# Start of a fused attention and MLP kernel: diagonal table, v and q's sums of batch 0 issued sooner, the first weight's magnitudes in h's buffers, products of constants in TensorE's planned gaps

## The chip, the cores and the metric

The kernel runs on one NeuronCore of a Trainium2 chip. A core has five engines that run at the same time, each through a queue of its own in order: TensorE (PE, matrix products; its weight loads, PEld, overlap with them), VectorE (DVE), ScalarE (ACT), GpSimd (POOL) and SyncE (SP), which here issues all DMAs. They wait for one another through semaphores. The time is that of one execution on the device, in microseconds; the median of several executions counts. One further execution is recorded by the hardware profiler.

## The reference

For a batch of 8 and 8 heads of 576 tokens by 64, a Nystroem attention with 32 landmarks (means over 18 tokens each of q and k), its output as 512 columns x; then x plus the real part of a two-dimensional Fourier transform of x, a normalisation, and a two-layer MLP whose input is added again.

```
q_lm, k_lm = means of 18 tokens
A, Bm, C = softmax(q k_lm'), softmax(q_lm k_lm'), softmax(q_lm k')
Z = Bm' / (norms);  6 times: Z = 2 Z - Z Bm Z
x = A Z C v
u = x + Re(fft(fft(x, tokens), columns))
un = (u - mean) / sqrt(var + 1e-6)
out = u + relu(un @ w1) @ w2          # w1 512x2048, w2 2048x512
```

## The kernel before, in words

All products are of float16 pairs (a high and a low part, three products for one) or of float32. Two things have to happen before the MLP can run. The weights arrive as 64-bit floats: each weight has 16 pieces of 128 by 512. ACT forms a piece's magnitudes (`prepare`), DVE takes the float32 out of the bits in three instructions, ACT sums its magnitudes for a bound (the inner `bound`), and when all 16 have a bound, one scale for the weight is worked out (`scale`) and each piece is halved into high and low part (`halve`, ACT then DVE, in place, one slot below where it lay). And batch 0 has to go through the attention (`tokens`, `landmarks`), the transform (`mix`) and the normalisation (`norm`); its normalised rows are transposed by DMA into `unT`. The MLP (`mlp`) works on chunks of 256 rows: the first layer gives tiles `h`, the second (`second`) adds them up in two PSUM tiles `acc0` and `acc1`. The second layer of chunk 0 needs the halved second weight.

The program is a planner in Python (`run`): attention, weights and MLP are generators, taken in this order of priority, and each yields how long it means to wait. The planner keeps a time of its own, `now`, that moves on by the reckoned length of each product (`mm`, `tr`; at full clock) and, when every generator waits, jumps to the first that is due. What it emits is PE's order, fixed by hand (`manual_schedule`). The order on the other engines' queues is worked out afterwards by the framework, from the order of emission, the dependencies and its own reckoning of times, so an instruction emitted early may come later on its engine.

Loads: `load(0)`, called in the constructor, issues k and q of batch 0 for two groups of heads, then for each group `EARLY` = 4 pieces of the first weight and v. The other pieces are issued by `weights`, one ahead of `prepare`. The small constants are issued around it, the diagonal table `diag32` and the transform's tables (`t1`, `t1t`, `t2`) after it. The buffers `big` (8), `mid` (7), `row` (6) and `h` (4) are rings that several uses share; a new tile waits until an earlier one of its ring is free. In `tokens`, per group: DVE forms landmark sums `lm`, ACT sums of magnitudes of q (`amax`), and DVE the masked sums `qbd`; then a scale `kb`, a product with ones, and the splits of q. In `landmarks`, the table `diag32` enters where `nrm` is formed, and again in the first step of the iteration.

Of the kernel before, what the change touches and what calls it, by code (L numbers as in the profile page):

```python
# [2 lines left out]

# [1 line left out]

# [5 lines left out]
F32 = mybir.dt.float32  # L11
F16 = mybir.dt.float16
# [6 lines left out]
P = 128  # L19
# [3 lines left out]
SEG = 73  # L23
# [7 lines left out]
LAG = 2  # L31


AHEAD, PREP, EARLY = 1, 4, 4

MARGIN, NM, AM, M0 = 1.5, 2.0, 2.0, 0.2

# [90 lines left out]
class Kernel:  # L128
    def __init__(self, ctx, tc, NB, q, k, v, w1, w2, t1, t1t, t2, diag, mask, out):
        self.tc, self.nc, self.NB = tc, tc.nc, NB  # L130
        self.q, self.k, self.v, self.w1, self.w2, self.out = q, k, v, w1, w2, out
        nc = self.nc
        pool = lambda n, b: ctx.enter_context(tc.tile_pool(name=n, bufs=b))
        psum = lambda n, b: ctx.enter_context(tc.tile_pool(name=n, bufs=b, space=bass.MemoryType.PSUM))
        self.cp, self.wk, self.sm = pool("cp", 1), pool("wk", 1), pool("sm", 2)
        self.ps_at, self.ps_h, self.ps_o = psum("ps_at", 8 - PSH - TCH), psum("ps_h", PSH), psum("ps_o", 1)
        self.loads = {}
        self.now, self.there, self.read, self.used = 0.0, {}, {}, []
        self.V, self.A = Timed(self, nc.vector, 0.07, 1.04e-3, 0.52e-3), Timed(self, nc.scalar, 0.2, 0.83e-3, 0.83e-3)
        self.G = Timed(self, nc.gpsimd, 0.1, 2.6e-3, 2.8e-3)  # L140
        self.dma_free = 2.0

        def const(src, shape, dtype, name):
            t = self.cp.tile(shape, dtype, name=name)
            nc.sync.dma_start(t, src)
            return t

        self.wraw, self.raw_there = [], []
        self.whole = [self.cp.tile([P, NF + 1, 512], F32, name=f"w{w}") for w in range(2)]
        self.mask = const(mask, [P, 6], F32, "mask")  # L150
        self.load(0)
        self.mask4, self.mask2 = self.mask[:, 0:4], self.mask[:, 4:6]
        self.diag32 = const(diag, [P, 32], F32, "diag")
        self.ident = self.cp.tile([P, P], F32, name="ident")
        make_identity(nc, self.ident)
        self.ones = self.cp.tile([P, P], F32, name="ones")
        nc.vector.memset(self.ones, 1.0)
        self.ones16 = self.cp.tile([P, P], BF16, name="ones16")
        nc.vector.memset(self.ones16, 1.0)
        self.ones_bd = self.cp.tile([P, 4, 32], F32, name="ones_bd")  # L160
        nc.vector.tensor_copy(self.ones_bd, self.mask4.unsqueeze(2).broadcast_to([P, 4, 32]))
        self.mhalf = self.cp.tile([P, 2], F32, name="mhalf")
        nc.vector.memset(self.mhalf, -0.5)

        self.Wx = self.cp.tile([P, 2, 2, 256], F16, name="Wx")
        self.Wt = self.cp.tile([P, 2, 4, 64], F16, name="Wt")
        for t in (self.Wx, self.Wt):
            nc.gpsimd.memset(t, 0.0)
        self.t1 = const(t1, [P, 4, 2, 160], F16, "t1")
        self.t1t = const(t1t, [P, 2, 2, 320], F16, "t1t")  # L170
        self.t2 = const(t2, [P, 4, 2, 2, NC], F16, "t2")
        self.arrival(1.7)
# [40 lines left out]
    def split(self, hi, lo, src, scale):  # L213
        self.A.activation(hi, src, AF.Copy, scale=scale)
        self.V.scalar_tensor_tensor(lo, src, scale, hi, ALU.mult, ALU.subtract)
# [34 lines left out]
    def weights(self):  # L250
# [12 lines left out]
        def prepare(i):  # L263


            mag = self.row(512)
            A.activation(mag, self.wraw[i].rearrange("p (m x) -> p m x", x=2)[:, :, 1].bitcast(F32), AF.Abs, scale=2.0**-112)
            mags.append(mag)

        def bound(i):  # L270
# [104 lines left out]
    def tokens(self, b, st):  # L375
# [10 lines left out]
        for g in range(2):  # L386
            kf, qf = loads[g][0][:, 0 : 2 * S], loads[g][1][:, 0:NQ]
            V.tensor_reduce(lm[:, g, 64:128], kf.rearrange("p (m t) -> p m t", t=18), AX.X, ALU.add)

            lv = lm[:, g, 0:64].rearrange("p (x o m) -> p x o m", o=2, m=8)  # L390
            qv = qf.rearrange("p (x o t) -> p x o t", o=2, t=2 * SEG)
            for o in range(2):
                V.tensor_reduce(lv[:, :, o], qv[:, :, o, o : o + 144].rearrange("p x (m t) -> p x m t", t=18), AX.X, ALU.add)
            qhs.append(self.big().bitcast(F16))
            A.activation(qhs[g][:, 0:NQ], qf, AF.Abs, accum_out=am[:, g : g + 1])
            for h2 in range(2):
                ms, cols = self.mask2[:, h2 : h2 + 1], slice(32 * h2, 32 * h2 + 32)
                V.tensor_scalar(
                    qbd[:, 2 * g : 2 * g + 2, cols], lm[:, g, 0:64].rearrange("p (r m) -> p r m", r=2), ms, None, ALU.mult
                )  # L400
            yield self.till(qbd)
# [4 lines left out]
        eq, rq = self.power(am[:, 0:2], 2, 2.0**-13, "aq")  # L406
        kb = self.small(2, "kb", BF16)
        V.tensor_tensor(kb, am[:, 2:4], eq, ALU.mult)
        yield self.till(kb, more=AM)
        ek, rk = self.bound(kb, 2, 2.0**-13, "ak")  # L410
        sc = self.small(4, "sc")
# [6 lines left out]
        for h2 in range(2):  # L418
# [2 lines left out]
                kbd[..., cols].rearrange("p g y r m -> p (g y r) m"), klm.rearrange("p g y (r m) -> p (g y r) m", r=2),  # L421
                ms, None, ALU.mult,
            )
        qm = [h[:, 0:2048].rearrange("p (y r t) -> p y r t", y=2, r=2) for h in qhs]
        qr = [h[:, 2048:2304].rearrange("p (y r t) -> p y r t", y=2, r=2) for h in qhs]
        for g in range(2):
            qs = loads[g][1][:, 0:NQ].rearrange("p (x t) -> p x t", t=2 * SEG)
            for t, a, w in ((qm[g], 1, 128), (qr[g], 129, 16)):
                split(
                    *(t[:, y].rearrange("p r (s t) -> p (r s) t", t=w) for y in range(2)),  # L430
                    qs[:, :, a : a + w], rq[:, g : g + 1],
                )
            if g == 0:
                yield self.till(qhs[0], kbd)
        while b == 1 and self.seconds < NF // 2 - HB:
            yield 0.5

# [275 lines left out]
    def mix(self, b, st, WC, Wx, x2, x13):  # L713
# [5 lines left out]
        for nt in range(3):  # L719
# [44 lines left out]
            if nt < 2 or b2 == 1:  # L764
                yield from self.norm(b, uts)

    def u_tile(self):
        self.ulive += 1
        return self.wk.tile([P, DM], F32, name="u", bufs=UB)
# [64 lines left out]
    def mlp(self):  # L834
# [4 lines left out]

        def second(ch, i, h):  # L840
            if i == 0:
                acc[:] = [self.ps_o.tile([P, DM], F32, name=f"acc{t}") for t in range(TCH)]
            while self.split_w[1] < 2 * i + 2:
                yield 0.5
            yield self.till(h)
            for t in range(TCH):
                for x in range(2):
                    f = 2 * i + x
                    mm3(acc[t], lambda y: h[:, y, x, P * t : P * t + P], lambda y: self.w2s[f][:, y, :],
                        start=(f == 0), stop=(f == NF - 1))  # L850
                    yield 0.0
                if f == NF - 1:
                    u = self.utiles[TCH * ch + t]
                    V.scalar_tensor_tensor(u, acc[t], self.inv2, u, ALU.mult, ALU.add)
                    nc.sync.dma_start(self.out[(TCH * ch + t) * P : (TCH * ch + t + 1) * P, :], u)
                    self.ufree.append(self.now + 4.5)

            self.seconds += 1

        for ch in range(self.NB // 2 * 9 // TCH):  # L860
# [6 lines left out]
            for i in range(NF // 2):  # L867
                while self.split_w[0] < 2 * i + 2:
                    yield 0.5
                ps = self.ps_h.tile([P, 512], F32, name="h")  # L870
                for x in range(2):
                    for c in range(KT):
                        mm3(ps[:, n * x : n * x + n], lambda y: self.w1s[2 * i + x][:, y, c, :], lambda y: unT[:, y, c, :],
                            start=(c == 0), stop=(c == KT - 1))
                        if c % 2:
                            yield 0.0
                if ch > 0 or i >= NF // 2 - HB:
                    h = self.wk.tile([P, 2, 2, n], F16, name="h", bufs=HB)
                else:

                    h = self.mid().bitcast(F16)[:, 0 : 4 * n].rearrange("p (y x t) -> p y x t", y=2, x=2)
                hv = [h[:, y].rearrange("p x t -> p (x t)") for y in range(2)]
                A.activation(hv[0], ps, AF.Relu)
                V.scalar_tensor_tensor(hv[1], ps, 0.0, hv[0], ALU.max, ALU.subtract)
                while len(late) >= LAG and (ch > 0 or self.split_w[1] >= 2 * late[0][1] + 2):
                    yield from second(*late.pop(0))
                late.append((ch, i, h))
# [14 lines left out]
    def run(self):  # L902
# [9 lines left out]
        with self.tc.manual_schedule(engines={mybir.EngineType.PE}):  # L912
            while self.threads:
# [6 lines left out]
                            self.threads.remove(th)  # L920
                        break
                else:
                    self.now = min(t[1] for t in self.threads)
                assert self.now < 5000


# [65 lines left out]
```

## Time and profile before

| | us |
|---|---|
| median of 3 executions | 1054.99 |
| lowest, highest | 1053.08, 1055.08 |
| the profiled execution | 1054.7 |
| its span, first to last instruction | 1052.9 |
| PE busy | 966.5 |
| DVE busy | 627.3 |
| ACT busy | 347.3 |
| POOL busy | 146.7 |

The page gives busy time by engine, then 40 slices of the span (a digit is the busy share in tenths; PEclk is the clock granted to PE in tenths of full speed), the DMA queues, the chain that ended last, and groups of instructions. Other views of the same trace give an engine's waits, the instructions in order of time, and busy times for chosen stretches. The line numbers that instructions carry are mostly those of helpers (L123 for DVE, ACT and POOL, L201 and L206 for PE), so instructions are told apart by their tiles, written "out<-in". "at" is any PSUM tile of the attention; "w" the weights, "wsc" their scales, "wm" a weight's maximum.

### The profile page before, as it was taken

How to read it: one execution, taken by the hardware profiler on the slowest of the kernel's cores; microseconds unless marked ns; L12 is line 12 of the kernel's file. 1: busy time of each engine (PE TensorE's matmuls, PEld its weight loads, DVE VectorE, ACT ScalarE, POOL GpSimd, SP SyncE). 2: the span in 40 equal slices, each digit the busy share in tenths (PEclk: the TensorE clock that was granted, in tenths of full speed). 3: DMA queues.
4: the chain of work that ended last, by engine and by line, in shares of the span. 5: the costliest groups of instructions: out<-in, count | busy, mean ns of one | idle time of the engine just before them, and what ended most of it. 6: DMA issues, size and time to landing. Idle time of an engine off the chain costs nothing.

```text
span 1052.9 us, 19418 instructions
## 1 busy us (share of the span) xinstructions
PE 966.5 (92%) x7900; PEld 666.3 (63%) x7900; DVE 627.3 (60%) x1684; ACT 347.3 (33%) x771; POOL 146.7 (14%) x161
## 2 busy tenths in 40 slices
PE   1556678899999999999999999999999999999998
PEld 0434434567776677766776677767766677676665
DVE  7888898779553665538745674687451754441111
ACT  3567755333231422223332332233222322111110
POOL 0101102034011030112302130214010130110000
PEclk8577889999999999999999999999999999999999
DMA  9564412123411123112502250125021110120000
GB/s 324 183 220 141 136 48 94 45 42 58 162 21 31 37 69 135 21 31 46 177 9 50 36 168 17 46 41 167 28 41 21 46 24 21 21 50 21 1 21 21
DMA packets 102122, 75.63 MB, mean 72 GB/s; under 512 B 72464, under 2 KB 90896, under 8 KB 101904
## 3 DMA queue, kind: packets, MB, share of 16 engines
q1 hardware_dynamic: 102032, 74.39, 25.0%
q8 instruction: 62, 1.02, 0.4%
q14 instruction: 28, 0.23, 0.1%
HBM read 48.02 MB, written 9.44 MB: 55 GB/s over the span
## 4 chain that ended last, share of the span: by engine, by line
PE 81%; DVE 10%; issue 4%; ACT 3%; DMA 1%; POOL 1%; SPq 0%; POOLq 0%; ACTq 0%; DVEq 0%
PE h L201 34%; PE acc L201 33%; PE at L201 14%; DVE w L123 2%; DVE mid L123 1%; DVE row L123 1%; DVE lm L123 1%; ACT mid L123 1%; DVE big L123 1%; ACT w L123 1%; DMA big<-q_dram 1%; ACT big L123 1%; DVE asum L123 0%; DMA unT<-row 0%; POOL mid L123 0%
## 5 line engine op out<-in xcount | busy, mean ns | idle before, releaser
L201 PE MATMUL h<-unT,w 128*128 128x256 f16 x3456 | 416.9, 275 | 16.8 <-DVE w L123 7.5
L201 PEld LDWEIGHTS <-w 128*128 128x128 f16 x3456 | 337.4, 99 | 92.6 <-DVE w L123 10.6
L201 PE MATMUL acc<-w,h 128*128 128x512 f16 x1680 | 393.6, 380 | 0.0
L201 PEld LDWEIGHTS <-h 128*128 128x128 f16 x1680 | 162.7, 98 | 163.3 <-issue 4.5
L123 DVE SCALAR_TENSOR_TENSOR h<-h 128x512 f16<-128x512 f32 x140 | 95.9, 685 | 205.3 <-ACT h L123 204.7
L123 ACT ACTIVATE h<-h 128x512 f16<-128x512 f32 x140 | 83.1, 594 | 287.4 <-PE h L201 275.4
L123 POOL TENSOR_TENSOR mid<-mid 128x256 f32<-128x256 f32 (+2 forms) x44 | 48.8, 1118 | 178.7 <-ACT mid L123 128.6
L123 POOL TENSOR_TENSOR r<-ve,mhalf 128x2 f32<-128x2 f32 (+1 forms) x20 | 13.8, 688 | 410.4 <-DVE ve L123 405.4
L123 POOL TENSOR_TENSOR row<-row 128x512 f16<-128x512 f32 (+1 forms) x44 | 47.7, 1100 | 43.2 <-ACT row L123 43.2
L123 DVE TENSOR_REDUCE lm<-big 128x32 f32<-128x576 f32 (+1 forms) x48 | 44.2, 945 | 13.9 <-DMA big<-k_dram 11.0
L201 PEld LDWEIGHTS <-mid 128*128 128x128 f16 x432 | 39.5, 102 | 19.1 <-issue 9.4
L123 ACT CAST row<-row 128x512 f16<-128x512 f32 (+1 forms) x44 | 23.3, 556 | 82.4 <-DVE row L123 82.2
L201 PEld LDWEIGHTS <-big 128*128 128x128 f16 (+1 forms) x768 | 41.5, 105 | 10.9 <-issue 2.2
L123 DVE TENSOR_TENSOR mid<-mid 128x256 f32<-128x256 f32 (+1 forms) x60 | 40.7, 693 | 12.2 <-DMA mid<-mid 9.7
L123 DVE SCALAR_TENSOR_TENSOR row<-at,scw,row 128x262 f32<-128x262 f32 (+1 forms) x48 | 21.4, 486 | 39.1 <-ACT row L123 19.2
L123 ACT ACTIVATE row<-w 128x512 f32<-128x512 f32 x54 | 33.8, 639 | 19.2 <-DMA w<-w_dram 9.8
L123 DVE SCALAR_TENSOR_TENSOR u<-at,scw,row 128x128 f32<-128x128 f32 (+3 forms) x120 | 39.0, 388 | 0.5 <-DMA out_dram<-u 0.5
L201 PE MATMUL at<-RE,E 128*128 128x96 f32 (+1 forms) x192 | 30.2, 281 | 8.3 <-DVE RE L123 8.3
L201 PEld LDWEIGHTS at<-RE,E 128*128 128x128 f32 x192 | 26.6, 196 | 14.2 <-DVE RE L123 6.0
L201 PE MATMUL at<-mid,big 128*128 128x262 f16 (+1 forms) x288 | 33.9, 288 | 0.0
L123 DVE SCALAR_TENSOR_TENSOR u<-acc,wsc,u 128x512 f32<-128x512 f32 x36 | 26.6, 747 | 11.8 <-PE acc L201 11.7
L123 POOL TENSOR_TENSOR mid<-mid,asum 128x512 f32<-128x512 f32 x14 | 15.2, 1090 | 123.6 <-DVE asum L123 113.3
(164 smaller groups left out, 932.8 us busy)
## 6 DMA issues: line engine op xcount, KB each, us to landing
w<-w_dram SPq DMA_DIRECT2D x22, 512.0 KB, 8.9
big<-v_dram SPq DMA_DIRECT2D x16, 640.0 KB, 9.2
big<-q_dram SPq DMA_DIRECT2D x16, 584.0 KB, 5.9
big<-k_dram SPq DMA_DIRECT2D x16, 576.0 KB, 4.5
out_dram<-u SPq DMA_DIRECT2D x36, 256.0 KB, 2.0
big<-w_dram SPq DMA_DIRECT2D x10, 512.0 KB, 6.1
unT<-row SPq DMA_TRANSPOSE x72, 2.5
t<-t_dram SPq DMA_DIRECT2D x1, 1048.0 KB, 9.5
```

The costliest lines, as they stand in the source:

```text
L123: return call(out, *args, **kw)
L201: self.nc.tensor.matmul(out, a, b, start=start, stop=stop, skip_group_check=True)
```

## The change

Five edits.

```
-AHEAD, PREP, EARLY = 1, 4, 4
+AHEAD, PREP, EARLY = 1, 4, 2
...
         self.mask = const(mask, [P, 6], F32, "mask")
+        self.diag32 = const(diag, [P, 32], F32, "diag")
         self.load(0)
         self.mask4, self.mask2 = self.mask[:, 0:4], self.mask[:, 4:6]
-        self.diag32 = const(diag, [P, 32], F32, "diag")
```

The diagonal table is issued ahead of batch 0's loads, and only two pieces of the first weight ahead of each v; the next four follow the tables.

```
-            mag = self.row(512)
-            A.activation(mag, self.wraw[i]..., AF.Abs, scale=2.0**-112)
+            mag = self.h_tile().rearrange("p y x t -> p (y x t)").bitcast(F32) if i < NF else self.row(512)
+            with self.tc.issue_after(self.first_sums) if i < NF // 2 else nullcontext():
+                A.activation(mag, self.wraw[i]..., AF.Abs, scale=2.0**-112)
...
-            A.activation(qhs[g][:, 0:NQ], qf, AF.Abs, accum_out=am[:, g : g + 1])
+            ins = A.activation(qhs[g][:, 0:NQ], qf, AF.Abs, accum_out=am[:, g : g + 1])
+            if b == 0:
+                self.first_sums = ins.ins
...
+    def h_tile(self):
+        return self.wk.tile([P, 2, 2, TCH * P], F16, name="h", bufs=HB)
```

The first weight's magnitudes use tiles of h's ring, and the first eight of them come on ACT's queue behind the sums of q of batch 0 that have been emitted by then. `mlp` takes its h tiles from `h_tile` too.

```
         V.tensor_tensor(kb, am[:, 2:4], eq, ALU.mult)
+        ... split_q(g): the two splits of group g, formerly in a loop behind kbd
+        split_q(0)
         yield self.till(kb, more=AM)
...
-        for g in range(2):
-            ...
-            if g == 0:
-                yield self.till(qhs[0], kbd)
+        split_q(1)
+        yield self.till(qhs[0], kbd)
```

The first half of q is split ahead of the product that kb is for, in every batch.

```
+        self.idle = self.cp.tile([P, 256], BF16, name="idle")
+        nc.vector.memset(self.idle, 1.0)
+        self.spare = self.ps_o.tile([P, DM], F32, name="acc0")
...
             if i == 0:
+                self.spare = None
                 acc[:] = [self.ps_o.tile([P, DM], F32, name=f"acc{t}") for t in range(TCH)]
...
                 else:
-                    self.now = min(t[1] for t in self.threads)
+                    until = min(t[1] for t in self.threads)
+                    while self.spare is not None and until - self.now > 0.25:
+                        self.mm(self.spare[:, 0:256], self.ones16, self.idle)
+                    self.now = until
```

Where the planner's time jumps by more than 0.25 us, products of a 128x128 tile of ones with 256 columns of ones are emitted for the time of the jump, into the PSUM tile that `acc0` uses later and that nobody reads until then. The last ones come before the second layer's first call.

More of the change, by code (lines that the diff above doesn't have):

```diff
@@ L1 @@
 import math
-from contextlib import ExitStack
+from contextlib import ExitStack, nullcontext
 import numpy as np
@@ L263, in prepare @@
         def prepare(i):
-            mag = self.row(512)
-            A.activation(mag, self.wraw[i].rearrange("p (m x) -> p m x", x=2)[:, :, 1].bitcast(F32), AF.Abs, scale=2.0**-112)
+            mag = self.h_tile().rearrange("p y x t -> p (y x t)").bitcast(F32) if i < NF else self.row(512)
+            with self.tc.issue_after(self.first_sums) if i < NF // 2 else nullcontext():
+                A.activation(mag, self.wraw[i].rearrange("p (m x) -> p m x", x=2)[:, :, 1].bitcast(F32), AF.Abs, scale=2.0**-112)
             mags.append(mag)
@@ L408, in tokens, with split_q @@
         V.tensor_tensor(kb, am[:, 2:4], eq, ALU.mult)
+        qm = [h[:, 0:2048].rearrange("p (y r t) -> p y r t", y=2, r=2) for h in qhs]
+        qr = [h[:, 2048:2304].rearrange("p (y r t) -> p y r t", y=2, r=2) for h in qhs]
+        def split_q(g):
+            qs = loads[g][1][:, 0:NQ].rearrange("p (x t) -> p x t", t=2 * SEG)
+            for t, a, w in ((qm[g], 1, 128), (qr[g], 129, 16)):
+                split(
+                    *(t[:, y].rearrange("p r (s t) -> p (r s) t", t=w) for y in range(2)),
+                    qs[:, :, a : a + w], rq[:, g : g + 1],
+                )
+        split_q(0)
         yield self.till(kb, more=AM)
@@ L423, in tokens @@
             )
-        qm = [h[:, 0:2048].rearrange("p (y r t) -> p y r t", y=2, r=2) for h in qhs]
-        qr = [h[:, 2048:2304].rearrange("p (y r t) -> p y r t", y=2, r=2) for h in qhs]
-        for g in range(2):
[L427 to L432, printed above, removed]
-            if g == 0:
-                yield self.till(qhs[0], kbd)
+        split_q(1)
+        yield self.till(qhs[0], kbd)
         while b == 1 and self.seconds < NF // 2 - HB:
@@ L877, in mlp @@
                 if ch > 0 or i >= NF // 2 - HB:
-                    h = self.wk.tile([P, 2, 2, n], F16, name="h", bufs=HB)
+                    h = self.h_tile()
                 else:
```

## The prediction

> **What bounds the kernel now.** I read the page's 40 slices first, to see where TensorE (PE) isn't full.
>
> ```profile
> span 1052.9 us, 19418 instructions
> PE   1556678899999999999999999999999999999998
> DVE  7888898779553665538745674687451754441111
> PEclk8577889999999999999999999999999999999999
> ```
>
> From the eighth slice on PE is full; before, it is half full at a reduced clock, and DVE is the fuller engine. The windows view prices those stages (columns: stretch, length, busy time of PE, weight loads, DVE, ACT and POOL, granted clock, DMA share, GB/s; the last row is the same view for DVE alone).
>
> ```profile
> 0.00:140.00 140.00, 73.75 (x568) 52.18 (x569) 118.15 (x301) 87.92 (x202) 14.64 (x19) 0.76 0.60 193
> 140.00:172.00 32.00, 23.30 (x157) 11.42 (x156) 26.95 (x88) 17.36 (x35) 0.00 (x0) 0.82 0.17 56
> 250.00:1053.00 803.00, 796.90 (x6551) 553.21 (x6548) 418.47 (x1110) 210.84 (x464) 113.32 (x122) 1.00 0.20 53
> 5.25:140.00 134.75, 117.61 (x297) 0.75 0.60 194
> ```
>
> After 250 us PE is busy 796.9 of 803 at full clock, with work that the change doesn't touch: an earlier start of that stage moves the end by as much, and nothing else does. Two views in order of time show when it can start.
>
> ```profile
> 139.64 0.16 DVE L123 TENSOR_REDUCE wm<-wmax 128x1 f32<-128x16 f32 x1
> 144.67 0.72 ACT L123 ACTIVATE w<-w,wsc 128x512 f16<-128x512 f32 x1 [4.35 <-DVE wsc L123]
> 158.32 0.72 ACT L123 ACTIVATE w<-w,wsc 128x512 f16<-128x512 f32 x1 [0.82 <-DVE w L123]
> 159.07 0.75 DVE L123 SCALAR_TENSOR_TENSOR w<-w,wsc 128x512 f16<-128x512 f32 x1 [0.79 <-ACT w L123]
> 170.07 0.72 ACT L123 ACTIVATE w<-w,wsc 128x512 f16<-128x512 f32 x1 [1.27 <-DVE w L123]
> ```
>
> The maximum of the second weight is taken at 139.64, when its last piece is decoded. Then its pieces are halved one after another, ACT waiting for DVE and DVE for ACT (each writes a slot that the one before still reads), to 170.07: a chain of some 25 us (170.07 - 144.67) that hangs on 139.64 and that no edit shortens. Up to 139.64 DVE sets the pace: from its first load (5.25) to 140 it works 117.61 of 134.75 us. So the gain, if there is one, is what goes of DVE's 134.75 - 117.61 = 17.1 us of idle time. Its waits up to 140, by the view of waits (us in total, times, longest):
>
> ```profile
> DVE mid L123 <- ACT mid L123: 3.1, 2, 1.9
> DVE row L123 <- POOL row L123: 2.6, 2, 1.6
> DVE w L123 <- ACT w L123: 2.0, 2, 1.8
> DVE cmx L123 <- PE at L201: 1.4, 3, 0.5
> DVE wm L123 <- PE at L201: 1.1, 1, 1.1
> DVE RE L123 <- PE at L201: 0.7, 1, 0.7
> DVE E L123 <- PE at L201: 0.7, 1, 0.7
> DVE row L123 <- ACT row L123: 0.5, 1, 0.5
> DVE amx L123 <- PE at L201: 0.4, 1, 0.4
> ```
>
> **The change part by part.** *The multiplied constants.* Wherever the planner leaves PE idle for over 0.25 us before the second layer begins, products of 256 columns of ones fill the gap. What that buys is the clock.
>
> ```profile
> 12.62 0.43 PE L201 MATMUL at<-lm,qbd 128*64 128x32 f32 x4 [2.92 <-DVE qbd L123]
> 12.86 4.09 PE L201 MATMUL at<-big,qbd 128*64 128x288 f32 x16
> 235.06 2.14 PE L201 MATMUL at<-big,qbd 128*64 128x288 f32 x16
> 95.23 4.58 PE L201 MATMUL h<-unT,w 128*128 128x256 f16 x23 [0.83 <-DMA unT<-row]
> 226.40 2.62 PE h L201 x24
> 99.00:100.00 1.00, 1.00 (x13) 0.71 (x12) 0.00 (x0) 0.15 (x1) 0.38 (x1) 0.92 0.00 0
> 43.00:44.00 1.00, 0.59 (x6) 0.42 (x4) 0.94 (x6) 0.60 (x1) 0.00 (x0) 1.00 0.00 0
> 45.00:46.00 1.00, 0.73 (x4) 0.76 (x5) 1.00 (x6) 0.00 (x0) 0.29 (x1) 0.50 0.00 0
> ```
>
> The same 16 products take 4.09 us early and 2.14 later: the early ones ran at half clock, though the page's first slice shows 8. A product of 256 columns takes 4.58 / 23 = 0.20 us slow and 2.62 / 24 = 0.11 fast; the fast clock comes some 4 us into a burst (95.23 to 99) and was gone again at 45, with PE some 0.6 busy at 43. If PE stays fast, DVE's waits on it shrink. The two waits on "mid" (3.1 us) stand behind first-layer bursts like that of 95.23, which shortens by half its 4.58; I take 2.5 (from 0 to 3.1). Those on E, wm and RE at 60 us (0.7, 1.1, and shares of the small ACT copies between, the 0.5 of row among them) stand behind short products; of the 2.3 I take 1.9 (0 to 2.3). Those on RE at 37 us and amx (0.7 + 0.4) stand behind the scores: 0.8 (0 to 1.1). Those on cmx (1.4) I count at 0 (below). Sum: 2.5 + 1.9 + 0.8 = 5.2 us gained, between 0 and 7.9.
>
> The page "TensorE: Matmul & The Clock Gate" of the Trainium skill (Part 1) has PE throttle only after a whole idle window of about 3.4 us and speed up after a busy one. By that rule PE should have stayed fast from 43 to 45, and few constants would do; the rows disagree, since a PE 0.6 busy was throttled there. The sum would be the same -5.2 by either.
>
> What the constants cost: their operand is set by DVE behind ones_bd.
>
> ```profile
> 2.52 0.23 DVE L161 COPY ones_bd<-mask 128x128 f32<-128x128 f32 x1 [1.37 <-DMA mask<-mask_dram]
> ```
>
> So PE can begin at about 2.52 + 0.23 + 0.2 = 2.9 us (the set of 128x256 taken at the size of that copy), in time in which DVE waits for its first load: nothing on DVE. But PE is then behind. Filling the 12.62 us before the first products that wait for DVE takes 12.62 / 0.11 = 115 constants: 25 of them slow (5 us at 0.20), 90 fast (9.9 us), so they end at 2.9 + 5 + 9.9 = 17.8, 5.2 us late. The 16 products behind then take 2.14 in place of 4.09, which leaves 3.2 us. I take that as hidden, since batch 0's chain has more slack than that (next part) and DVE has pieces to decode meanwhile; the gain on cmx is given up for it. Without that cover it is a rival. In all, at most (140 - 73.75) / 0.11 = 602 constants, 66 us of PE's idle time; none comes after the second layer's first call, and the slow products there are covered by the halving chain (0; the bound is what the clock of 0.82 costs in the 32 us from 140 on, 0.18 x 32 = 5.8 us).
>
> *Diagonal table, q's sums, v.*
>
> ```profile
> 0.74 0.39 SPq L145 DMA_DIRECT2D mask<-mask_dram  x1
> 1.19 0.42 SPq L361 DMA_DIRECT2D big<-k_dram  x1
> 17.60 0.68 DVE L123 SCALAR_TENSOR_TENSOR w<-w,row 128x512 int32<-128x512 int32 x1
> 19.22 0.21 DVE L123 TENSOR_REDUCE rs<-nrm 128x2 f32<-128x64 f32 x1
> 25.66 1.16 ACT L123 ACTIVATE big<-big 128x1168 f16<-128x1168 f32 x1
> 28.59 0.14 DVE L123 TENSOR_TENSOR kb<-amax,aq_e 128x2 bf16<-128x2 f32 x1
> 29.72 0.22 DVE L123 TENSOR_TENSOR nrm<-diag,rs 128x64 f32<-128x64 f32 x1
> 36.23 1.08 PE L201 MATMUL at<-big,mid 128*32 128x64 f32 x31
> 29.93 0.69 DVE L123 SCALAR_TENSOR_TENSOR w<-w,row 128x512 int32<-128x512 int32 x1
> ```
>
> The table now goes ahead of k and q on SP's queue: their issue moves by 1.19 - 0.74 = 0.45 us, and DVE's first work with it: +0.45. It landed so late that nrm waited from 19.4 (the end of rs) to 29.72, 10 us, and q's sums ran at 25.66, behind magnitudes of the first weight on ACT, so kb came at 28.59. With both early, batch 0's chain can run some 10 us sooner. That isn't 10 us of time: from 17.60 to 29.93 DVE decoded seven pieces, so it only does its work in another order. Next late in the place of table and sums are the splits of q (a pair on DVE for each half), of which the change takes the first half ahead of the wait for kb's product. I take 0; the bounds are -2 (a chain that is done sooner leaves fewer steps in which DVE waits) and the loss of the next point. v was needed at 36.23, behind a chain that started at 28.59; 10 us sooner it needs v1 at 26, which it gets, two pieces of weight being gone from ahead of each v: 0.
>
> The edge that holds the first eight magnitudes behind q's sums makes ACT wait for q: behind it stand those magnitudes, and DVE's decoding behind them. the second half of q is reduced and masked ahead of the products of 12.62, so two sums of 1.16 end at about 13 at the latest, and the first piece was decoded with the row of 17.60: 0, with 1.16 as the other end.
>
> *Four pieces later.* Pieces 4 to 7 of the first weight are issued behind v and the tables and not before v1, so the second v and all tables stand ahead of piece 4 now. By 30 us DVE had decoded seven pieces (17.60 is the end of the first, 29.93 that of the last), three of them from piece 4 on, each at most three rows like these: 3 x 3 x 0.69, up to 6.2 us of work in hand gone, against q's splits and the rest of batch 0's chain that are early now. I take 0; bounds 0 and +6.2.
>
> *Magnitudes in h's buffers.* Four buffers of their own in place of a share of six; ACT is busy 87.9 of 140 us and DVE waits 0.5 us for such a row: 0, from -0.5 to +1 (at most four in flight, not five).
>
> **Sum:** -5.2 + 0.45 = -4.7. The profiled execution took 1054.7 us (span 1052.9, 1.8 around it), 0.3 under the median of 1054.99: 1054.7 - 4.7 = 1050.0.
>
> **The rivals.** 0.2% is 2.1 us, about what a measurement can tell from no change.
>
> *The constants make PE late (slower).* PE takes its queue in order and every planned gap is full, so the 5.2 us by which the first constants run late are never made up: each later product starts as late against the plan. For: the count above; the planner reckons with full clock and constants from time 0, and the trace shows neither. Against: batch 0's chain was itself 10 us late. It decides from the point where DVE has no decoded piece ready and waits for a product. Then the gain is lost and 5.2 + 0.45 comes on top: 1060.4.
>
> *The waits change their owner.* DVE's queue has an order of its own; where PE is sooner, it waits for ACT or POOL instead (4 of the 9 rows above are theirs, 2.6 and 2.0 among them), or PE idles beyond the plan where DVE is late, and is slow again. By the page named above an idle window of 3.4 us would be enough for that; the trace's row at 45 says that less is enough. Gain and 0.45 cancel: 1054.5.
>
> *More holes close.* Batch 0's chain done early also takes the waits on POOL and ACT (2.6 + 2.0 + 0.5) and the 2 us of the chain's bound away: -4.7 - 7.1, 1042.9.
>
> **How the numbers follow.** Forecast 1050.0: 0.45. PE late, 1060.4: 0.25. Owner changed, 1054.5: 0.18. More holes, 1042.9: 0.12. The range of 1041 to 1062 takes in both outer cases with their unknowns and leaves less than 2 in 10. Faster: 0.12 and nearly all of the forecast's 0.45, less its small ends, 0.55; within 0.2%: the third case, 0.17; slower: PE late and the bad ends of the others, 0.28.
>
> **What would show it.** The clock in the rows of 20 to 140 us near 1.0 and the first-layer bursts at 0.11 us a product, or that part is wrong. The maximum of the second weight (wm) at about 135 and not 139.64, DVE's idle time from its first load to there near 12 us and not 17, and an end that moved by as much. kb and nrm some 10 us sooner. If products with their operands long there stand behind rows of constants while DVE waits for "at" or "h", PE is late. If DVE idles between 14 and 26 us for a piece, the four later pieces cost. If wm moved and the end didn't, the halving chain isn't the gate that I take it for.

## The result, and the profile after

| | before | after |
|---|---|---|
| median, us | 1055.03 | 1088.18 |
| lowest to highest (4 runs each) | 1053.08 to 1055.76 | 1087.11 to 1092.19 |
| span of the profiled execution | 1052.9 | 1086.9 |

The ratio is 1.0322 (95%: 1.0305 to 1.0339): 33 us slower, where 5 us faster was forecast, and outside the range. The page of the kernel after, first part and slices:

```profile
span 1086.9 us, 19869 instructions
PE 997.2 (92%) x8117; PEld 688.8 (63%) x8117; DVE 636.6 (59%) x1685; ACT 349.0 (32%) x771; POOL 146.8 (14%) x161
PE   5664978898999999999999989997999999999998
PEclk8886989998999999999899999998999999999999
```

Early on PE is fuller now (5664 in place of 1556), but there are new notches later, at slices 10, 24 and 28, and PEclk, full from slice 7 on before, has some too, at 10, 20 and 28. The windows view of the kernel after, columns as in the prediction, says which stage lost:

```profile
0.00:140.00 140.00, 91.37 (x783) 69.49 (x783) 123.71 (x302) 87.73 (x202) 14.13 (x19) 0.82 0.60 194
140.00:172.00 32.00, 22.58 (x155) 11.00 (x156) 27.07 (x87) 17.21 (x34) 0.00 (x0) 0.84 0.17 56
250.00:1087.00 837.00, 810.36 (x6524) 558.22 (x6521) 422.80 (x1111) 213.95 (x465) 116.12 (x123) 0.98 0.18 51
```

From 250 us to the end, PE idles 837 - 810.36 = 26.6 us where it idled 803 - 796.9 = 6.1 before: 20.5 more. It is also busy 13.5 us longer (810.36 - 796.9), at a mean clock of 0.98 where it was 1.00. 20.5 + 13.5 = 34.0 is the whole difference of the spans (1086.9 - 1052.9). So, taken together, the start neither won nor lost; the loss lies in the stage that the prediction took as full and untouched. PE's waits from 240 us on, by the view of waits, first after and then before (us in total, times, longest):

```profile
PE at L205 <- DVE RE L123: 21.6, 11, 7.2
```

```profile
PE at L201 <- DVE RE L123: 1.1, 1, 1.1
```

21.6 - 1.1 = 20.5: all the added idle time is one wait, for "RE", DVE's scaling in the iteration for Z of `landmarks`. The longest, beside the same place of the same batch before. PE in order of time, before:

```profile
704.41 0.86 PE L201 MATMUL at<-kbd,big 128*128 128x64 f16 x24
...
707.08 2.75 PE L201 MATMUL acc<-w,h 128*128 128x512 f16 x12
709.66 0.86 PE L201 MATMUL at<-kbd,big 128*128 128x64 f16 x24
712.12 0.47 PE L201 MATMUL at<-kbd,big 128*64 128x64 f16 x12
714.49 0.58 PE L201 MATMUL at<-RE,E 128*128 128x96 f32 x4
```

and DVE before:

```profile
713.22 0.59 DVE L123 TENSOR_SCALAR RE<-at,cr,ci 128x64 f32<-128x64 f32 x2
716.08 0.36 DVE L123 TENSOR_TENSOR mid<-mid 128x256 f32<-128x256 f32 x1
```

The scores q k_lm' of this batch come in three units, of 24, 24 and 12 products "at<-kbd,big", some 5 and 2.5 us apart (in every second batch the last two come together, 7.0 us behind the first), and DVE works on the first unit's maxima and sums while PE does something else. Both scalings RE are done (713.22) before the first of the sums "mid<-mid" that prepare the transform (716.08), and PE takes its product with RE without a wait. After, all engines in order of time:

```profile
727.53 1.96 PE L205 MATMUL at<-kbd,big 128*128 128x64 f16 x60
738.37 0.81 PE L205 MATMUL acc<-w,h 128*128 128x512 f16 x3
739.24 2.12 DVE L123 TENSOR_TENSOR mid<-mid 128x256 f32<-128x256 f32 x3
744.50 1.15 POOL L123 TENSOR_TENSOR mid<-mid 128x512 f16<-128x512 f32 x1
745.68 0.43 DVE L123 TENSOR_TENSOR mid<-mid 128x256 f32<-128x256 f32 x1 [4.33 <-POOL mid L123]
746.02 0.34 DVE L123 TENSOR_SCALAR RE<-at,cr,ci 128x64 f32<-128x64 f32 x1
746.42 1.33 PE L205 MATMUL at<-RE,E 128*128 128x96 f32 x4 [7.24 <-DVE RE L123]
747.54 3.59 PE L205 MATMUL acc<-w,h 128*128 128x512 f16 x9
```

All 60 products run in one go. RE's scaling now stands behind four sums on DVE. The fourth waits 4.33 us for POOL, which works through the units' scalings and differences one after another until 744.50 + 1.15 = 745.65. What RE reads of PE's had long been there: PE had had nothing to do since 739.18 (738.37 + 0.81). RE waits for nothing of its own; it waits because of where it stands. And behind the stall nine products of 512 columns take 3.59 us, 0.40 each; before, twelve took 2.75 at 707.08, 0.23 each. The clock in this stretch, by the windows view (columns: stretch, length, PE busy, clock, DMA share, GB/s):

```profile
742.00:743.00 1.00, 0.00 (x0) 1.00 0.28 55
744.00:745.00 1.00, 0.00 (x0) 0.50 0.25 51
749.00:750.00 1.00, 1.00 (x4) 0.50 0.03 4
751.00:752.00 1.00, 1.00 (x11) 1.00 0.00 0
```

The clock halves some 4.5 us after PE's last product and comes back some 4 us after the next. That is the other part of the loss: a stall of 7.24 us also makes the next 4 us of work take about twice as long. By the page "TensorE: Matmul & The Clock Gate" of the Trainium skill (Part 1) a window of about 3.4 us idle throttles PE and one of about 3.4 us busy releases it; the rows of this stall agree with that in size.

In the other five batches of this stage the waits are shorter and come in pairs, one for each of the two scalings. The shortest pair before a slow stretch:

```profile
390.26 0.46 PE L205 MATMUL at<-RE,E 128*128 128x96 f32 x2 [0.97 <-DVE RE L123]
391.71 0.46 PE L205 MATMUL at<-RE,E 128*128 128x96 f32 x2 [0.99 <-DVE RE L123]
```

Neither wait is over 1 us, and yet the granted clock is 0.56 in the microsecond from 392, 0.50 in the next two and 0.73 from 395. PE was busy 1.0 of the 3 us from 389 to 392. Neither wait makes 3.4 us, nor do both together, so these rows don't agree with that page of the Trainium skill. Four of the five pairs are followed by such a stretch; the one at 880 (1.21 and 0.99 us) isn't. Summed over the single microseconds from 250 us on, the part of the clock that wasn't granted, times PE's busy time, gives 11.1 of the 13.5 us; the rest is open.

Every batch of this stage loses time. The first product with landmarks of a batch ("at<-lm,qbd"), early and late, before and after:

```profile
234.81 0.42 PE L201 MATMUL at<-lm,qbd 128*64 128x32 f32 x8
824.10 0.43 PE L201 MATMUL at<-lm,qbd 128*64 128x32 f32 x8
```

```profile
234.66 0.43 PE L205 MATMUL at<-lm,qbd 128*64 128x32 f32 x8
855.65 0.42 PE L205 MATMUL at<-lm,qbd 128*64 128x32 f32 x8
```

Level at the first (-0.15 us), 31.6 us behind at the last. In between it grows batch by batch (7.7, 11.6, 17.5, 23.1).

### The profile page after: what moved, and what is told of

The parts are those of the page before. It is cut to its first block, busy times and chain, and to the rows that moved or that the text cites. A ratio compares the mean times of both kernels' runs of the same rounds, so it can differ in the third digit from the quotient of the medians.

```text
span 1086.9 us, 19869 instructions
## 1 busy us (share of the span) xinstructions
PE 997.2 (92%) x8117; PEld 688.8 (63%) x8117; DVE 636.6 (59%) x1685; ACT 349.0 (32%) x771; POOL 146.8 (14%) x161
## 4 chain that ended last, share of the span: by engine, by line
PE 46%; issue 29%; DVE 13%; POOL 4%; ACT 3%; DMA 3%; SPq 1%; POOLq 0%; DVEq 0%; ACTq 0%
PE acc L205 20%; PE h L205 19%; PE at L205 7%; DVE mid L123 4%; POOL row L123 2%; DVE w L123 2%; DMA mid<-mid 2%; POOL mid L123 1%; DVE row L123 1%; DVE asum L123 1%; SPq L646 1%; DVE lm L123 1%; ACT row L123 1%; DVE h L123 1%; DVE amx L123 1%
## 5 line engine op out<-in xcount | busy, mean ns | idle before, releaser
L205 PE MATMUL acc<-w,h 128*128 128x512 f16 x1680 | 401.3, 384 | 0.0
L205 PEld LDWEIGHTS <-h 128*128 128x128 f16 x1680 | 164.9, 100 | 165.4 <-issue 11.1
L205 PE MATMUL at<-RE,E 128*128 128x96 f32 (+1 forms) x192 | 33.7, 297 | 27.2 <-DVE RE L123 27.1
L123 DVE TENSOR_TENSOR mid<-mid 128x256 f32<-128x256 f32 (+1 forms) x60 | 42.5, 718 | 20.5 <-POOL mid L123 11.6
L205 PEld LDWEIGHTS <-mid 128*128 128x128 f16 x432 | 38.4, 101 | 20.2 <-issue 10.8
L205 PEld LDWEIGHTS <-big 128*128 128x128 f16 (+1 forms) x768 | 39.3, 102 | 10.1 <-issue 3.0
L205 PE MATMUL acc<-idle,ones 128*128 128x256 bf16 x217 | 34.4, 313 | 1.5 <-DVE idle L164 1.5
L205 PEld LDWEIGHTS <-ones 128*128 128x128 bf16 x233 | 25.2, 111 | 14.9 <-DVE kb L123 6.6
```

Of the source, the lines that this page charges most:

```text
L123: return call(out, *args, **kw)
L205: self.nc.tensor.matmul(out, a, b, start=start, stop=stop, skip_group_check=True)
```

## The experiments

Ratios are to the kernel before on the same chip, with the 95% interval. "wm" is when the second weight's maximum is taken (139.64 before).

| kernel | median, us | ratio | PE's waits for RE, us | wm, us |
|---|---|---|---|---|
| after | 1088.18 | 1.0322 (1.0305 to 1.0339) | 21.6 | 139.86 |
| e1_only_split | 1104.37 | 1.0462 (1.0445 to 1.0480) | 25.2 | 147.68 |
| e2_no_split | 1055.14 | 1.0010 (0.9999 to 1.0021) | 1.8 | 138.62 |
| e3_only_idle | 1052.68 | 0.9977 (0.9967 to 0.9988) | 1.8 | 135.55 |
| e4_no_idle | 1094.48 | 1.0379 (1.0354 to 1.0404) | 24.9 | 139.47 |
| e5_both_ahead | 1092.26 | 1.0360 (1.0323 to 1.0397) | 17.9 | 146.20 |
| e6_second_behind | 1056.19 | 1.0010 (0.9999 to 1.0020) | 2.4 | 139.59 |
| e7_re_first | 1071.92 | 1.0154 (1.0135 to 1.0174) | 12.7 | 141.20 |
| e8_batch0_only | 1056.47 | 1.0012 (0.9999 to 1.0026) | 0.3 | 140.76 |
| e9_early4 | 1056.18 | 1.0018 (1.0008 to 1.0027) | 0.2 | 140.31 |
| e10_idle_diag_issue | 1055.85 | 1.0014 (1.0003 to 1.0025) | 1.8 | 140.45 |
| e11_idle_diag | 1052.50 | 0.9982 (0.9973 to 0.9992) | 0.8 | 136.85 |
| e12_idle_early | 1055.77 | 1.0012 (1.0002 to 1.0022) | 2.0 | 137.93 |

### Which edit costs

e1_only_split: the kernel before with the moved splits alone, in all batches.

```
         V.tensor_tensor(kb, am[:, 2:4], eq, ALU.mult)
+        split_q(0)
         yield self.till(kb, more=AM)
...
-        for g in range(2):
...
-            if g == 0:
-                yield self.till(qhs[0], kbd)
+        split_q(1)
+        yield self.till(qhs[0], kbd)
```

> The kernel before with one part of the change alone: both splits of q's order moved (first half ahead of kb's product, second ahead of the wait), in all 8 batches; no constants, no other part. Theory A (the moved splits change DVE's order in every batch, so that RE's scaling stands behind the sums that wait for POOL, and PE waits for RE once a batch): 1075 to 1090 us, and PE's waits for RE from 250 us on near the 21.6 us of the changed kernel, against 1.1 before. Theory B (the constants make PE late and the lag is never made up): 1053 to 1057, waits for RE near 1.

e2_no_split: the kernel after with the splits as they were before; the other edits stay.

> The changed kernel with q's splits back where they were before, all else of the change kept, the constants too. Theory A: the late loss is gone, 1045 to 1058 us, PE's waits for RE from 250 us on under 3 us. Theory B: 1080 to 1090 as the changed kernel.

e3_only_idle: the kernel before with the multiplied constants alone.

```
+        self.idle = self.cp.tile([P, 256], BF16, name="idle")
+        nc.vector.memset(self.idle, 1.0)
+        self.spare = self.ps_o.tile([P, DM], F32, name="acc0")
...
-                    self.now = min(t[1] for t in self.threads)
+                    until = min(t[1] for t in self.threads)
+                    while self.spare is not None and until - self.now > 0.25:
+                        self.mm(self.spare[:, 0:256], self.ones16, self.idle)
+                    self.now = until
```

> The kernel before with the constants alone. Theory A: 1048 to 1056 us (the constants keep the clock up and cost little). Theory B: 1070 to 1090.

e4_no_idle: the kernel after without them.

> The changed kernel without the constants, all else kept. Theory A: 1080 to 1095 us, as slow as the changed kernel or a little slower. Theory B: 1050 to 1058.

The splits alone lose more than the whole change and more than was expected (1.0462, 1104 us), and without them the loss is gone (1.0010). The constants alone gain 0.23%, and inside the changed kernel they are worth 1.0379 - 1.0322, some 6 us. In e1 the maximum wm comes 8.0 us later than before as well: batch 0 pays for the splits too, and in the kernel after the other edits hide that.

### Which line of the splits

The diff does two things to the splits: the first half goes ahead of the wait for kb's product, and the wait that stood between the halves goes behind both. e5_both_ahead: the kernel before with the second of these alone.

```
-            if g == 0:
-                yield self.till(qhs[0], kbd)
+        yield self.till(qhs[0], kbd)
```

> The kernel before with one line moved: the wait that stood between the splits of q's two halves now stands behind both; the splits stay behind kbd where they were. Theory C (the lost wait between the halves lets all three units of the scores be emitted at once, which puts their sums ahead of RE on DVE): 1085 to 1105 us, PE's waits for RE from 250 us on over 18. Rival D (it is the first half's place ahead of kb's product, which delays the key scale): 1052 to 1058, waits under 4.

e6_second_behind: the kernel after with that undone, the first half still ahead.

```
-        split_q(1)
-        yield self.till(qhs[0], kbd)
+        yield self.till(qhs[0], kbd)
+        split_q(1)
```

> The changed kernel with the second half of q split behind the wait again (the first half stays ahead of kb's product). Theory C: most of the loss is gone; RE stands behind the first unit's two sums still in some batches, so 1055 to 1068 us, PE's waits for RE from 250 us on 2 to 10. Rival D: 1080 to 1090 as the changed kernel.

e8_batch0_only: the kernel after with both splits moved in batch 0 alone.

```
-        split_q(0)
+        if b == 0:
+            split_q(0)
...
+        if b == 0:
+            split_q(1)
+            yield self.till(qhs[0], kbd)
+        else:
+            split_q(0)
+            yield self.till(qhs[0], kbd)
+            split_q(1)
```

> The changed kernel with q's splits moved in batch 0 alone. By theory C the late loss is gone: 1048 to 1055 us. If the splits of batch 0 gain nothing at the start either, it is as the run without any moved split (1055.1).

It is the wait. One line moved in the kernel before costs 3.6%, and moved back in the kernel after brings 1.0010 (2.4 us of waits for RE in all, none over 0.8). PE's waits from 240 us on in e5:

```profile
PE at L201 <- DVE RE L123: 17.9, 11, 3.0
```

The wait costs nothing in itself. While its generator waits, the planner emits other work, and so it keeps the second and third units of scores apart from the first. The traces show how far: from 240 us on the second unit comes 5.3 or 7.0 us behind the first in the kernel before and 5.3 in e6, but 1.4 to 2.0 in e5, and in the kernel after and in e1 all 60 products run in one go. So the first half's place has a share too: with the wait gone, it closes the gap that e5 still has, and e1 is some 11 us slower than e5. With the wait there (e6) it costs nothing to be seen. e8 takes the loss away too, so it lies in the batches from 1 on; its 1056.5 is within the noise of e2's 1055.1 and missed its expectation (up to 1055) by little.

### Where on DVE

If only the place of RE on DVE's queue mattered, it would be enough to hold the sums back. e7_re_first: the kernel after, with the sums of batches from 2 on ordered behind the second scaling RE.

```
-                    V.tensor_tensor(F1[...], ae[:, 0:256], ae[:, 256:512], op)
+                    f1i = V.tensor_tensor(F1[...], ae[:, 0:256], ae[:, 256:512], op)
+                    if b >= 2:
+                        self.behind(st, f1i.ins)
...
-            V.tensor_scalar(RE[:, g, 32:96], ...)
+            rei = V.tensor_scalar(RE[:, g, 32:96], ...)
+            if b >= 2 and g == 1:
+                st["re"] = rei.ins
+                for f1i in st.pop("f1", []):
+                    self.behind(st, f1i)
```

> The changed kernel with one more edit: from batch 2 on, DVE's sums and differences of the scores are queued behind RE's second scaling; PE's order is the changed kernel's, product for product. Theory E (the loss is RE's place on DVE's queue, behind sums that wait for POOL): 1053 to 1062 us, PE's waits for RE from 250 us on under 4. Rival F (PE's own order, the product of v 8 us behind the scores, costs the time): 1075 or more, and the waits for RE stay over 12.

Half of it came true: 16 of the 33 us are back, but neither the full return nor the low waits that were expected. Its waits on PE:

```profile
PE at L204 <- DVE RE L123: 12.7, 9, 2.6
```

Its DVE and PE in order of time:

```profile
727.58 0.56 DVE L123 TENSOR_SCALAR RE<-at,cr,ci 128x64 f32<-128x64 f32 x2
728.06 4.73 DVE L123 TENSOR_TENSOR mid<-mid 128x256 f32<-128x256 f32 x5
733.75 0.42 DVE L123 TENSOR_TENSOR E<-at,mask 128x256 f32<-128x256 f32 x1
736.73 0.29 DVE L123 TENSOR_TENSOR RE<-RE,at 128x128 f32<-128x128 f32 x1 [2.57 <-ACT RE L123]
```

```profile
737.08 0.69 PE L204 MATMUL at<-RE,E 128*128 128x96 f32 x4 [2.56 <-DVE RE L123]
```

RE's scaling goes first now, and the bunch of sums (4.73 us in one piece) comes behind it. The stall has moved one step of the iteration on, and to another queue. The sums aren't what the next product waits for: E, behind them, is ready at 734.17 (733.75 + 0.42), before PE runs out of work at 734.52 (733.06 + 1.46). What comes late is the new RE, and DVE waits 2.57 us for ACT's copy into it. On ACT that copy starts at 736.50, straight behind a cast at 735.97 that prepares the transform and had waited 1.95 us for POOL. It is so in six of e7's nine waits, 9.8 of the 12.7 us. In the kernel before, the sums lie between the steps, one or two at a time, and the same copy behind the same kind of cast makes PE wait once, for 1.1 us. So RE's place on DVE explains the long stall, and what follows from the bunch on POOL and ACT explains that a shorter one is left. No wait of e7 is longer than 2.6 us, and its mean clock in this stage is 1.00 again, with one slow stretch, behind the 2.56 us wait (0.50 from 739 to 741):

```profile
250.00:1070.50 820.50, 802.50 (x6537) 555.66 (x6534) 426.76 (x1113) 213.66 (x465) 113.82 (x123) 1.00 0.19 52
```

PE idles 18.0 us here (820.5 - 802.5), against 6.1 before and 26.6 after, and is busy 5.6 us longer than before, against 13.5. So most of the half-clock part is gone: by the same sum as above it is 1.7 us here. What the rest of the 5.6 is stays open.

### Where the gain of the constants goes

Without the splits, all other edits together (e2, 1.0010) do worse than the constants alone (e3, 0.9977). e9_early4 is e2 with `EARLY` back at 4:

> The changed kernel without the moved splits and with four pieces ahead of each v again: constants, diagonal table first, magnitudes in h's buffers behind q's sums. If the pieces that come later are what the other parts give back of the constants' gain (2.4 us between the run without moved splits and the run with the constants alone): 1051.5 to 1053.5 us, and wm near 136. If not: 1054.5 to 1056, wm near 138.6.

The first case missed: 1.0018, no better, with wm at 140.31. The next three add one edit to the constants at a time. e10_idle_diag_issue: constants, diagonal table first, and the edge behind q's sums.

> The kernel before with the constants, the diagonal table first and the magnitudes behind q's sums, in their old buffers and with four pieces ahead of each v. If batch 0's earlier chain is worth something, under 1052 us and the fastest; if it only does DVE's work in another order, 1052 to 1054 as with the constants alone; if the edge behind q's sums costs, 1054.5 or more.

e11_idle_diag: the same without the edge.

> The kernel before with the constants and the diagonal table first, nothing else. If the edge behind q's sums is what takes the constants' gain back: 1051.5 to 1053.5 us, wm near 136. If the table's place is (its 0.45 us and what follows in DVE's order): 1054.5 to 1056.5, wm near 140.

e12_idle_early: constants and `EARLY` = 2.

> The kernel before with the constants and two pieces ahead of each v in place of four, nothing else. If fewer early pieces cost nothing: 1051.5 to 1053.5 us as with the constants alone, or better; if DVE lacks pieces to decode near 20 us, 1054 to 1058 with idle time there.

The table costs nothing to be seen (0.9982 beside 0.9977). The edge takes the gain back (1.0014 beside 0.9982, some 3.4 us), and so does `EARLY` = 2 (1.0012 beside 0.9977, some 3.7). The two don't add: e2 has both and 1.0010. For e12 part of the place can be read: a pair of slow decoding steps at 102 us (next section) adds some 1.7 us that e3 doesn't have there, and its wm comes 2.4 us later than e3's. The idle time near 20 us that was expected is small: between 14 and 26 us DVE idles 1.6 us, against 0.5 in e3. In e10 the wait of DVE for q's sums is new, 1.5 us, and waits on PE that e11 had shortened are back; that is read from one profile and not shown by a further run. The magnitudes in h's buffers were never run alone.

The two fastest kernels are e3 and e11, at 1052.7 and 1052.5: 0.2% below the kernel before, just clear of it by their intervals.

## Why the prediction was wrong

**The step that failed** is the one on q's splits, with the sentence that it leaned on. The prediction said that PE's work after 250 us is "work that the change doesn't touch", and of the splits that the change "takes the first half ahead of the wait for kb's product. I take 0", priced between -2 and the next point's loss, for batch 0. But `tokens` runs for every batch, and beside the move of the first half the diff has a second move, of the wait that stood between the halves. It was not priced. e5 gives that line alone 1.0360 and e6, without it, 1.0010. In its place the runs showed units of scores that run closer together or in one go, and 20.5 us more of waits for RE and 13.5 us more of busy time, most of it work at half clock behind them. No rival had the place: "PE late" and "owner changed" both lie in the start. The second names the shape of what happened (PE idles where DVE is late, and is slow again), but it was priced there, at no more than the gain. The stage from 250 us on had its own sign of danger in the prediction's rows: with PE busy 796.9 of 803, any order that makes PE wait there is paid in full.

**The constants** were right in mechanism and smaller in size. Priced at -5.2 us; e3 measures them alone. Its maximum and its last halving on ACT, and DVE's waits to 140 us:

```profile
135.55 0.15 DVE L123 TENSOR_REDUCE wm<-wmax 128x1 f32<-128x16 f32 x1
171.78 0.72 ACT L123 ACTIVATE w<-w,wsc 128x512 f16<-128x512 f32 x1 [1.21 <-DVE w L123]
```

```profile
DVE row L123 <- POOL row L123: 1.6, 1, 1.6
DVE wm L123 <- PE at L204: 0.9, 1, 0.9
DVE cmx L123 <- PE at L204: 0.5, 1, 0.5
DVE mid L123 <- ACT mid L123: 0.5, 1, 0.5
```

wm comes 4.1 us sooner (135.55 for 139.64) where 5.2 was taken, and the time is 0.23% shorter. The waits on mid give 2.6 (3.1 to 0.5) where 2.5 was taken; cmx, counted at 0, gives 0.9; wm gives 0.2, so the 1.9 for the short products was too much. The clock that was to be "near 1.0" did not get there: 0.82 to 140 us in the kernel after and 0.85 in e3, from 0.76. My row at 43 us (PE 0.59 busy) was also the fullest of its neighbours: 0.05 at 41, 0.46 at 42 and 0.00 at 44, so PE was busy 1.1 of the 4 us in which it was throttled. The number of constants was far off, 217 in all against a bound of 602, and 41 at the start against 115:

```profile
1.47 7.04 PE L205 MATMUL acc<-idle,ones 128*128 128x256 bf16 x41 [1.47 <-DVE idle L164]
9.52 0.31 PE L205 MATMUL at<-lm,qbd 128*64 128x32 f32 x4 [1.01 <-DVE qbd L123]
```

They start at 1.47 and not at 2.9, since DVE set their operand ahead of ones_bd. They end at 8.51, and the first real products still wait 1.01 us for DVE. So the rival "PE late" falls: the planner's gap there was shorter than the trace's 12.62 us, which I had filled.

**The gate** is wm rather than the last halving, and the exchange rate doesn't hold. The halving runs longer than I read (my rows stopped at 172):

```profile
175.88 0.72 ACT L123 ACTIVATE w<-w,wsc 128x512 f16<-128x512 f32 x1 [1.21 <-DVE w L123]
```

That is before; in e3 the last one comes at 171.78, also 4.1 us sooner, and the batch that starts at 234.81 before starts 3.9 us sooner. In the kernel after the last one comes at 172.87, 3.0 us sooner, with wm level (139.86), and the batch starts level too (234.66). In all runs of the table this batch starts 94.6 to 96.2 us behind wm. So the start of the full stage goes with wm more closely than with the end of the halving; which step of the halving holds it is open. And "moves the end by as much" is wrong: the batch at 824.10 starts only 2.2 us sooner in e3, and the span is 2.1 shorter. Nearly half of the gain is given back in the full stage; where was not followed.

**DVE's idle time** from 5.25 to 140 us fell to the forecast's figure, 134.75 - 122.79 = 12.0 in the kernel after, and yet wm did not move (139.86). The agreement is luck: DVE's busy time rose by 5.2, with as many instructions (297). Groups by line of DVE in that stretch, after and before:

```profile
L123 DVE SCALAR_TENSOR_TENSOR w<-big,row 128x512 int32<-128x512 int32 x10 | 8.6, 864 | 0.0
```

```profile
L123 DVE SCALAR_TENSOR_TENSOR w<-big,row 128x512 int32<-128x512 int32 x10 | 6.8, 681 | 0.0
```

and all engines after, in order of time:

```profile
87.83 1.39 POOL L123 TENSOR_TENSOR row<-row 128x512 f16<-128x512 f32 x1 [4.65 <-ACT row L123]
88.12 1.64 DVE L123 SCALAR_TENSOR_TENSOR w<-big,row 128x512 int32<-128x512 int32 x1
89.94 1.43 POOL L123 TENSOR_TENSOR row<-row 128x512 f16<-128x512 f32 x1 [0.73 <-ACT row L123]
90.39 1.52 DVE L123 SCALAR_TENSOR_TENSOR w<-big,row 128x512 int32<-128x512 int32 x1
```

Two decoding steps that take 0.68 alone take 1.64 and 1.52 here, and both began while POOL was at work. Three more are as long in the same stretch (1.64 at 48.78, 1.53 at 102.93 and at 104.49). The five are 7.9 us in place of 3.4, 4.5 of the 5.2. Before, DVE stood idle for 2.6 us at POOL's rows instead. So idle time became longer instructions; this is the rival "the waits change their owner" in a form I hadn't seen: the new owner doesn't show as a wait. In e12 the pair at 102 us is long in the same way (1.53 and 1.52).

**The small terms.** The table first: k is issued at 1.66 for 1.19, +0.47 against +0.45. nrm comes at 18.90, 10.8 us sooner, as said. kb comes 6.2 us sooner, not some 10: q's sums ran at 19.42 and 20.58 on ACT and not by 13, since ACT's order put them behind C's exponentials. The edge, 0 with 1.16 as its other end, cost some 3.4 (e10 and e11): under-sized. The four later pieces, 0 between 0 and 6.2, cost some 3.7 beside the constants alone and nothing to be seen in e9. The sign for them that the prediction gave, DVE idle between 14 and 26 us for a piece, isn't there in the kernel after: DVE idles 3.1 us in that stretch, but its named waits there are for PE (cmx, 1.6) and for q's sums (1.5), not for a piece.

## What to carry to other kernels

In a kernel whose order is planned by program, a wait that an edit drops or moves is a change of order for everything emitted around it: list it as an edit of its own, and ask in which of the loop's passes it stands. A stage in which PE is 99% busy has no slack to hide a crowded queue of another engine; look there for what is emitted in one go and which short instruction that PE waits for will stand behind it, on whichever engine. And a fall in idle time is worth something only if the busy time stays: compare the mean duration of the same instructions too.

## What the runs showed of the hardware

Stalls of PE can cost more than their length, and they needn't be long. After the 7.24 us one the clock stayed at half until about 750.5; after the two of 0.97 and 0.99 us at 390, with 0.46 us of products between them, it was at half from 392 to 395.5. In e5, where no wait is longer than 3.0 us, that sum over the clock that wasn't granted, from 250 us on, is 11.7 us, as much as in the kernel after (11.1). In e7, whose waits stand alone and are 2.6 us at most, it is 1.7. The pair at 880 (1.21 and 0.99 us) left the clock at 1.00, so the length of the waits alone doesn't tell which of them cost it.

Constants keep the clock up only where the planner sees the gap. In the kernel after PE waited 12.0 us for DVE at 91.94, with nothing planned into that gap, and 22 products of the first layer then took 4.87 us, 0.22 each, as slow as before the change:

```profile
91.94 0.37 PE L210 MATMUL at<-ident,wm 128*1 128x128 f32 x1 [12.00 <-DVE w L123]
100.64 4.87 PE L205 MATMUL h<-unT,w 128*128 128x256 f16 x22 [0.89 <-DVE w L123]
```

And an instruction of DVE that meets one of POOL can take over twice its time (0.68 to 1.64 above). The page "SBUF — State Buffer" of the Trainium skill (section "Who interferes with whom") has the two share a port pair under an exclusive lock; the rows above agree. That it is this lock, and not another cause, no run here separates.
